# AdaLN block with spectral filter and SwiGLU: a rearranged prologue in place of a staged copy of the edge frequencies

## The chip, the cores and the metric

The kernel runs on one core of a Trainium2 chip. The metric is the device time of one execution in microseconds; the profile's own span (first to last instruction of the program) is 254.3 us where the run took 256.17 us. A core has five engines that this text names: TensorE (PE: matmuls and transposes), VectorE (DVE), ScalarE (ACT), GpSimd (POOL) and SyncE (SP), which here only issues transfers. Transfers (DMA) run on 16 DMA engines beside the compute engines.

## The reference

One token block `x` of 2048 x 640 in bfloat16 goes through two halves, each with a LayerNorm that is scaled and shifted by a vector computed from `c`. The first half filters the whole block in the frequency domain, the second is a SwiGLU feed-forward.

```python
mod = (silu(c) @ w_mod).reshape(1, 6, 1, 640)      # sa, ca, ga, sb, cb, gb
h = layernorm(x) * (1 + ca) + sa
X = rfft2(h, axes=(tokens, model))                 # 2048 x 321 frequencies
y = irfft2(X * (w_r + 1j * w_i), s=(2048, 640))
x = x + ga * y
h = layernorm(x) * (1 + cb) + sb
g = silu(h @ w_gate); u = h @ w_up                 # 640 -> 1728
x = x + gb * ((g * u) @ w_down)
```

## The kernel before

The Fourier transforms are matmuls against cosine and sine tables. The 2048 tokens stand in 16 tiles of 128 rows (`t` = 0..15). For each tile the kernel

- transposes x on TensorE (`t1`) and copies the result from PSUM to SBUF on ACT,
- takes the row statistics (`stats`), for tiles in `BN` with DVE's bn_stats, for the others with a Gram matrix of the transposed tile on TensorE (its diagonal is the sum of squares),
- transforms along the model dimension (`dfwd`), with tables `Rs` that carry the factor 1 + ca,
- subtracts the mean's share on DVE (`zout`), which needs a mean table `Cb`: the transform of a tile of ones,
- scales the token table by 1/std on GpSimd (`gscale`) and transforms along the token dimension (`s1`, lines 398 to 401, "first token matmul" is line 398), and ACT writes the result to `A_sb`.

[...] The start of the program, with the transfers:

```python
    nc.scalar.dma_start(c_row[:], c)
    wmca_v = wm_v[:, :, D:2 * D]
    nc.sync.dma_start(x_sb[:, 0:1, :], x_v[:, 0:1, :])
    nc.sync.dma_start(wm_ca[:, 0:3], wmca_v[:, 0:3])
    nc.scalar.dma_start(Rp[:, 4:5], R_dram[:, 4:5])
    nc.sync.dma_start(wm_ca[:, 3:5], wmca_v[:, 3:5])
    nc.sync.dma_start(Rp[:, 0:4], R_dram[:, 0:4])
    nc.sync.dma_start(x_sb[:, 1:2, :], x_v[:, 1:2, :])
    for xl, xh, gl, gh in ((2, 4, 0, 2), (4, 8, 2, NG9)):
        nc.sync.dma_start(x_sb[:, xl:xh, :], x_v[:, xl:xh, :])
        nc.sync.dma_start(Gtab[:, gl:gh], G_dram[:, gl:gh])
    ...
    def flip_edge(w, f):                                   # row 0 of the flipped table
        ncol = w.ap[0][0]
        nc.sync.dma_start(f[0:1, 0:NT - 1, :], bass.AP(...15 rows of 256...))
        nc.sync.dma_start(f[0:1, NT - 1, :], w[0:1, 65:65 + NW])
    def flip(w, f):                                        # rows 1..127, DRAM to DRAM, 1 MB
        nc.sync.dma_start(f[1:P].rearrange("p k l -> k p l"), bass.AP(...rows reversed...))

    nc.sync.dma_start(x_sb[:, 8:12, :], x_v[:, 8:12, :])
    flip(A_w_i, Wflip[0])
    nc.sync.dma_start(x_sb[:, 12:16, :], x_v[:, 12:16, :])
    flip_edge(A_w_i, Wflip[0])
    flip_edge(A_w_r, Wflip[1])
    flip(A_w_r, Wflip[1])
    nc.sync.dma_start(wm_sa[:], wm_v[:, :, 0:D])
    for i, w in ((0, A_w_i), (2, A_w_r)):
        nc.sync.dma_start(Wn[:, i, :, :], w.rearrange("(k2 k1) l -> k1 k2 l", k1=P)[:, :, 0:NW])
    nc.sync.dma_start(KS2, K_dram[:, 384:576])
    for i in range(2):
        nc.sync.dma_start(Wv[:, 2 * i, :, :], Wflip[i][:])
    nc.sync.dma_start(Ktab[:, 0:384], K_dram[:, 0:384])
    wm_m = wm_v[:, :, 2 * D:6 * D].rearrange("p k (i d) -> p k i d", i=4)
    nc.sync.dma_start(wm_r[:, :, 0, :], wm_m[:, :, 0, :])
```

The filter is needed in natural order (`Wn`) and with its frequencies reversed (`Wv`); the reversed copy is made in DRAM (`Wflip`) and then read back. Row 0 of it comes from other places of the input: these are the edges.

The scale vector and the first tiles:

```python
        t1(0)
        mps = psum[:, 7, 0:NC5]
        mod_cols(mps, wm_ca, range(0, 3))
        mod_cols(mps, wm_ca, range(3, 5))
        nc.vector.tensor_scalar_add(one_p_ca[:], mps, 1.0)
        R1 = Rs[:, 1].rearrange("p (h r) n -> p h (r n)", h=2)
        nc.vector.tensor_scalar_mul(R1[:, 0], R1[:, 0], one_p_ca[:, 4:5])
        nc.vector.tensor_scalar_mul(Rs[:, 0, 0, :], Rp[:, 0, :], one_p_ca[:, 0:1])
        nc.scalar.mul(Rs[:, 0, 1, :], Rp[:, 1, :], one_p_ca[:, 1:2])
        nc.vector.tensor_scalar_mul(R1[:, 1], R1[:, 1], one_p_ca[:, 4:5])
        nc.vector.tensor_scalar_mul(Rs[:, 0, 2, :], Rp[:, 2, :], one_p_ca[:, 2:3])
        nc.scalar.mul(Rs[:, 0, 3, :], Rp[:, 3, :], one_p_ca[:, 3:4])
    idle_pe(IDLE[2])
    t1(1)
    stats(0)
    dfwd(0)
    t1(2)
    stats(1)
    t1(3)
    cbz = zbank(1)
    dft_d(cbz, [ones[:]] * NC5, Rs)                        # mean table, TensorE
    stats(2)
    nc.scalar.mul(Cb[:]..., zview(cbz), 1.0)               # mean table, ACT (line 451)
    gscale(0)
    stats(3)
    zout(0)
    t1(4)
    dfwd(1)
    gscale(1)
    zout(1)
    for t in range(2, NT + 2):
        if t + 3 < NT:
            t1(t + 3)
        if t + 2 < NT:
            stats(t + 2)
        s1(t - 2, Zs.pop(t - 2), Gss.pop(t - 2))
        ...
        if t < NT:
            dfwd(t)
            zout(t)
        ...
```

The middle of the kernel goes over groups of frequencies: A is transposed (by TensorE for the first groups, by DMA transposes for the rest, line 504), transformed over the remaining 16 residues (`stage_a`), multiplied with the filter on DVE (`prod`, line 573), and brought back (`stage_b`, `stage_c`). `evac` copies the result from PSUM to `Em`. Group 4 holds the two edge frequencies 0 and 80:

```python
            B2b = rL.cut(4096 * bi, [16, 128]) if bi < 3 else rM.cut(6144, [16, 128])
            nc.sync.dma_start_transpose(B2b[:, :n, :], A_sb[:, l0:l0 + n, :, :, :].rearrange("p l t c r -> p l (t c r)"))
            for i in range(n):
                B2of[l0 + i] = (B2b, i, l0, n)

        t2_dma(0)
        t2_dma(1)
        t2_dma(2)
        nc.sync.dma_start(wm_r[:, :, 1:3, :], wm_m[:, :, 1:3, :])
        t2_dma(3)
        nc.sync.dma_start(wm_r[:, :, 3, :], wm_m[:, :, 3, :])
        nc.sync.dma_start(Htab[:], H_dram)
        nc.sync.dma_start(RI[:], RI_dram)
        ...
        def evac(u):
            g, l0 = units[u][0], groups[units[u][0]][0]
            if l0 == 0:
                edge = rY.cut(4096, [2, 128])
                nc.scalar.copy(edge[:], banks(6, 1, [4, 128])[:, 0:2, :])       # line 608
                for i in range(2):
                    nc.gpsimd.tensor_copy(Em[:, :, :, 64 * i].rearrange("p v q -> p q v"),
                                          edge[:, i, :].rearrange("p (q v) -> p q v", v=2))   # line 610
            ...
        for g in range(NG + 1):
            ...
            if g + 2 < NG:
                PPs[g + 2] = stage_a(g + 2)[0]     # from group 13 on with modulation matmuls (line 555)
            ...
            for u, gs in enumerate(units):
                if gs[-1] + (1 if gs[0] >= NG - 2 else 3 if gs[0] == 4 else 2) == g:
                    stage_c(u)
                    evac(u)
```

After that come the transform back to tokens, the second LayerNorm and the feed-forward, which the change does not touch.

Of the kernel before, what the change touches and what calls it, by code (L numbers as in the profile page):

```python
# [23 lines left out]
NG9 = 9  # L24
BN = (0, 4, 8, 14)
FLIP = (15, 14, 13, 12, 11, 10, 9)
# [129 lines left out]
def adaln_block_kernel(ctx, tc, A_x, A_w_r, A_w_i, B_x, B_w_gate, B_w_up, B_w_down, c, w_mod, out):  # L156
    nc = tc.nc
# [21 lines left out]
    rY = _Region(big, "rY", 7680, "Y")  # L179
# [31 lines left out]
    wm_ca = rM.cut(0, [NC5, D])  # L211
# [11 lines left out]
    Cb = rE.cut(o, [4, 162], F32); o += 2592  # L223
# [21 lines left out]
    wmca_v = wm_v[:, :, D:2 * D]  # L245
    nc.sync.dma_start(x_sb[:, 0:1, :], x_v[:, 0:1, :])
    nc.sync.dma_start(wm_ca[:, 0:3], wmca_v[:, 0:3])
    nc.scalar.dma_start(Rp[:, 4:5], R_dram[:, 4:5])
    nc.sync.dma_start(wm_ca[:, 3:5], wmca_v[:, 3:5])
    nc.sync.dma_start(Rp[:, 0:4], R_dram[:, 0:4])  # L250
# [22 lines left out]
    nc.sync.dma_start(x_sb[:, 12:16, :], x_v[:, 12:16, :])  # L273
    flip_edge(A_w_i, Wflip[0])
    flip_edge(A_w_r, Wflip[1])
    flip(A_w_r, Wflip[1])
    nc.sync.dma_start(wm_sa[:], wm_v[:, :, 0:D])
    for i, w in ((0, A_w_i), (2, A_w_r)):
        nc.sync.dma_start(Wn[:, i, :, :], w.rearrange("(k2 k1) l -> k1 k2 l", k1=P)[:, :, 0:NW])
    nc.sync.dma_start(KS2, K_dram[:, 384:576])  # L280
    for i in range(2):
# [44 lines left out]
    def zview(zps, M=P):  # L326
        return zps[0:M, :, 0:324]


    if True:  # L330
# [115 lines left out]
        stats(1)  # L446
        t1(3)
        cbz = zbank(1)
        dft_d(cbz, [ones[:]] * NC5, Rs)
        stats(2)  # L450
        nc.scalar.mul(Cb[:].rearrange("p (h r) n -> p h (r n)", h=2), zview(cbz), 1.0)
        gscale(0)
        stats(3)
        zout(0)
        t1(4)
# [3 lines left out]
        for t in range(2, NT + 2):  # L459
# [5 lines left out]
            if t == 14:  # L465
                sps = psum[:, 7, 400:400 + NL]
                for i in range(10):
                    r, c2 = i // 2, i % 2
# [28 lines left out]
    if True:  # L497
# [106 lines left out]
        def evac(u):  # L604
            g, l0 = units[u][0], groups[units[u][0]][0]
            if l0 == 0:
                edge = rY.cut(4096, [2, 128])
                nc.scalar.copy(edge[:], banks(6, 1, [4, 128])[:, 0:2, :])
                for i in range(2):
                    nc.gpsimd.tensor_copy(Em[:, :, :, 64 * i].rearrange("p v q -> p q v"),  # L610
                                          edge[:, i, :].rearrange("p (q v) -> p q v", v=2))
            elif g == NG - 2:
# [54 lines left out]
        for g in range(NG + 1):  # L667
# [16 lines left out]
            for u, gs in enumerate(units):  # L684
                if gs[-1] + (1 if gs[0] >= NG - 2 else 3 if gs[0] == 4 else 2) == g:
                    stage_c(u)
                    evac(u)
# [582 lines left out]
```

## Time and profile before

| | |
|---|---|
| time, median of 3 runs | 256.17 us (255.61 to 256.83) |
| span of the profiled run | 254.3 us, TensorE clock 1.00 |
| busy share: PE, DVE, ACT, POOL | 96%, 82%, 64%, 29% |
| DMA moved | 34.78 MB, mean 137 GB/s |
| forward transform ends (last write of A) | 37.9 us |
| middle, to the first matmul of the way back (line 645) | 65.1 us |
| rest: way back, second LayerNorm, feed-forward | to 254.3 us |

How to read the views: the page gives the busy time of each engine over the whole span and in 40 slices. The timeline lists instructions with start, length, engine, line, output and inputs; in brackets is how long the engine was idle before and what released it. The chain is followed back from the last instruction to what released each step. SPq is SyncE's queue: its entries are the issue of transfers, not the transfers. A landing is the time from issue to the arrival of all of it.

### The profile page before, as it was taken

How to read it: one execution, taken by the hardware profiler on the slowest of the kernel's cores; microseconds unless marked ns; L12 is line 12 of the kernel's file. 1: busy time of each engine (PE TensorE's matmuls, PEld its weight loads, DVE VectorE, ACT ScalarE, POOL GpSimd, SP SyncE). 2: the span in 40 equal slices, each digit the busy share in tenths (PEclk: the TensorE clock that was granted, in tenths of full speed). 3: DMA queues.
4: the chain of work that ended last, by engine and by line, in shares of the span. 5: the costliest groups of instructions: out<-in, count | busy, mean ns of one | idle time of the engine just before them, and what ended most of it. 6: DMA issues, size and time to landing. Idle time of an engine off the chain costs nothing.

```text
span 254.3 us, 6501 instructions
## 1 busy us (share of the span) xinstructions
PE 244.9 (96%) x2520; PEld 199.5 (78%) x2520; DVE 208.0 (82%) x521; ACT 163.7 (64%) x305; POOL 73.6 (29%) x117
## 2 busy tenths in 40 slices
PE   8899987999999999999999999999999999999984
PEld 3788856999788887788877678886668886679953
DVE  2898888888888897979997995879985788994793
ACT  3778656988778698578863477673356766235730
POOL 4387756764021805000004600001430000440021
PEclk9999999999999999999999999999999999999999
DMA  7989999999999899710005120002411000212001
GB/s 222 389 278 336 306 394 190 270 275 390 309 332 281 221 257 156 153 36 0 3 0 106 39 70 8 3 3 52 92 40 35 3 0 4 52 52 59 4 0 52
DMA packets 46588, 34.78 MB, mean 137 GB/s; under 512 B 22111, under 2 KB 43486, under 8 KB 46174
## 3 DMA queue, kind: packets, MB, share of 16 engines
q1 hardware_dynamic: 44892, 30.36, 43.2%
q0 software_dynamic: 1376, 3.93, 6.6%
q8 instruction: 19, 0.31, 0.5%
q10 hardware_dynamic: 290, 0.08, 0.1%
q14 instruction: 11, 0.09, 0.1%
HBM read 26.80 MB, written 4.72 MB: 124 GB/s over the span
## 4 chain that ended last, share of the span: by engine, by line
PE 69%; DVE 5%; ACT 4%; DMA 3%; SPq 2%; issue 1%; DVEq 0%; ACTq 0%
PE psum L1058 29%; PE psum L933 17%; PE psum L1031 8%; DMA rM<-in_w_mod_dram 3%; PE psum L645 3%; SPq L504 2%; PE psum L803 2%; PE psum L580 2%; PE psum L806 2%; PE psum L912 1%; PE psum L551 1%; DVE rA L898 1%; PE psum L601 1%; PE psum L1010 1%; PE psum L650 1%
## 5 line engine op out<-in xcount | busy, mean ns | idle before, releaser
L1058 PEld LDWEIGHTS <-rW 128*128 128x128 bf16 (+1 forms) x528 | 47.0, 98 | 5.9 <-issue 0.6
L949 POOL TENSOR_TENSOR rM<-rM,rL 128x320 f32<-128x320 f32 x7 | 6.2, 885 | 86.4 <-ACT rL L948 86.4
L1058 PE MATMUL psum<-rE,rW 128*128 128x256 f16 (+1 forms) x192 | 27.7, 259 | 0.2 <-ACT rH L1090 0.2
L1058 PE MATMUL psum<-rW 128*128 128x256 bf16 (+1 forms) x240 | 27.1, 259 | 0.0
L1058 PE MATMUL psum<-rY,rW 128*128 128x256 bf16 (+1 forms) x96 | 24.0, 259 | 0.0
L573 DVE TENSOR_TENSOR rM<-psum,rW 128x384 bf16<-128x384 f32 (+2 forms) x42 | 20.4, 542 | 3.7 <-PE psum L551 3.4
L933 PEld LDWEIGHTS <-rX 128*128 128x128 bf16 (+1 forms) x181 | 16.1, 97 | 9.2 <-issue 1.6
L1031 PE MATMUL psum<-rW 128*128 128x256 bf16 (+1 forms) x170 | 23.2, 291 | 0.0
L933 PEld LDWEIGHTS <-rE 128*128 128x128 f16 x168 | 16.4, 98 | 6.5 <-DVE rE L884 0.2
L933 PE MATMUL psum<-rE 128*128 128x320 f16 x126 | 20.4, 299 | 0.0
L933 PE MATMUL psum<-rA,rX 128*128 128x320 bf16 (+1 forms) x119 | 19.5, 301 | 0.8 <-DVE rX L1037 0.8
L1031 PEld LDWEIGHTS <-rW 128*128 128x128 bf16 x170 | 16.6, 98 | 3.8
L1058 PEld LDWEIGHTS <-rE 128*128 128x128 f16 x192 | 17.4, 98 | 2.3
L1108 DVE TENSOR_TENSOR rX<-rH,rL 128x512 bf16<-128x512 bf16 x21 | 8.9, 425 | 11.7 <-ACT rL L1106 11.5
L736 POOL TENSOR_TENSOR rstd<-rstd,mhalf 128x4 f32<-128x4 f32 (+2 forms) x4 | 4.7, 1187 | 44.8 <-DVE rstd L732 44.8
L1098 DVE TENSOR_TENSOR rX<-psum,rX 128x512 f32<-128x512 f32 x21 | 14.4, 688 | 3.2 <-ACT rX L1097 2.9
L1097 ACT COPY rX<-psum 128x512 f32<-128x512 f32 x21 | 12.3, 587 | 7.2 <-PE psum L1058 7.1
L1094 DVE TENSOR_TENSOR rH<-psum,rW 128x512 bf16<-128x512 f32 x21 | 14.5, 690 | 2.4 <-PE psum L1058 0.6
L1090 ACT COPY rH<-psum 128x512 f32<-128x512 f32 x21 | 12.2, 581 | 6.4 <-PE psum L1058 5.7
L1084 ACT COPY rW<-psum 128x512 f32<-128x512 f32 x21 | 12.3, 586 | 5.8 <-PE psum L1058 5.8
L390 DVE SCALAR_TENSOR_TENSOR rE<-rE,mv,psum 128x648 bf16<-128x648 f32 (+1 forms) x17 | 14.1, 841 | 2.0 <-PE psum L323 1.6
L1058 PE MATMUL psum<-rW,rE 128*128 128x256 bf16 (+1 forms) x96 | 15.1, 259 | 0.0
(203 smaller groups left out, 665.5 us busy)
## 6 DMA issues: line engine op xcount, KB each, us to landing
out_dram<-rA SPq DMA_DIRECT2D x31, 80.0 KB, 1.6
rM<-in_w_mod_dram SPq DMA_DIRECT2D x3, 800.0 KB, 9.2
rA<-in_B_w_down_dram SPq DMA_DIRECT2D x1, 2080.0 KB, 12.8
rX<-in_A_x_dram SPq DMA_DIRECT2D x3, 640.0 KB, 7.2
rM<-in_w_mod_dram SPq DMA_DIRECT2D x1, 1600.0 KB, 8.0
rY<-in_B_w_gate_dram POOLq DMA_DIRECT2D x2, 768.0 KB, 6.9
rW<-in_B_w_gate_dram SPq DMA_DIRECT2D x2, 640.0 KB, 7.0
rW<-in_B_w_up_dram SPq DMA_DIRECT2D x2, 640.0 KB, 8.0
```

The costliest lines, as they stand in the source:

```text
L390: nc.vector.scalar_tensor_tensor(Zv[:, h], Cv[:, h], mv[:, t, 0:1], zps[:, h], ALU.mult, ALU.subtract)
L573: nc.vector.tensor_tensor(PP[:, :, hl], xv[:, :, hl], in1, ALU.mult)
L645: nc.tensor.matmul(vps[:, r, :], lhsT=Em[:, v, 4 * t + r, :], rhs=Htab[:, t, v, :], start=(v == 0), stop=(v == 1))
L933: nc.tensor.matmul(o, lhsT=lhsT, rhs=rhs, start=start, stop=stop, skip_group_check=True)
L1031: nc.tensor.matmul(gu[u], lhsT=Wgu[:, u, c5, ff * 128:(ff + 1) * 128], rhs=h2T[:, :, c5, :], start=(c5 == 0), stop=(c5 == NC5 - 1))
L1058: nc.tensor.matmul(o[:, f], lhsT=w, rhs=b, start=(start and f == 0 and i == 0), stop=(stop and f == F - 1 and i == len(ops) - 1), skip_gro ...
L1084: nc.scalar.copy(c0, X)
L1090: nc.scalar.copy(c2, X)
L1094: nc.vector.tensor_tensor(c11, Z, c0, ALU.add)
L1097: nc.scalar.copy(c3, X)
L1098: nc.vector.tensor_tensor(c22, Y, c3, ALU.add)
L1108: nc.vector.tensor_tensor(ato, v4(c11), v4(g21), ALU.mult)
```

## The change

It has five parts.

1. The modulation weights for the scale (`wm_ca`) are issued from two queues, the second part from ACT's, to free SyncE for what follows.
2. The mean table is made ahead of the fourth transpose, and `zout(0)` stands ahead of `stats(3)`, so that the first token matmul can follow sooner.
3. Tile 14 takes its statistics from a Gram matrix, like the other tiles, which takes bn_stats off DVE.
4. The edges of the flipped filter are issued after the natural tables instead of between the flips.
5. The edge frequencies go from PSUM straight to `Em`, one by ACT and one by DVE, with a strided write, in place of one contiguous copy by ACT into SBUF and two strided copies from there by GpSimd; the unit is taken one group earlier.

```diff
@@ -22,7 +22,7 @@
 NC5 = 5
 NFC = 14
 NG9 = 9
-BN = (0, 4, 8, 14)
+BN = (0, 4, 8)
 FLIP = (15, 14, 13, 12, 11, 10, 9)
 EPS = 1e-5
 RC = 162
@@ -244,9 +244,9 @@
     nc.scalar.dma_start(c_row[:], c)
     wmca_v = wm_v[:, :, D:2 * D]
     nc.sync.dma_start(x_sb[:, 0:1, :], x_v[:, 0:1, :])
+    nc.scalar.dma_start(wm_ca[:, 3:5], wmca_v[:, 3:5])
     nc.sync.dma_start(wm_ca[:, 0:3], wmca_v[:, 0:3])
     nc.scalar.dma_start(Rp[:, 4:5], R_dram[:, 4:5])
-    nc.sync.dma_start(wm_ca[:, 3:5], wmca_v[:, 3:5])
     nc.sync.dma_start(Rp[:, 0:4], R_dram[:, 0:4])
     nc.sync.dma_start(x_sb[:, 1:2, :], x_v[:, 1:2, :])
     for xl, xh, gl, gh in ((2, 4, 0, 2), (4, 8, 2, NG9)):
@@ -271,12 +271,12 @@
     nc.sync.dma_start(x_sb[:, 8:12, :], x_v[:, 8:12, :])
     flip(A_w_i, Wflip[0])
     nc.sync.dma_start(x_sb[:, 12:16, :], x_v[:, 12:16, :])
-    flip_edge(A_w_i, Wflip[0])
-    flip_edge(A_w_r, Wflip[1])
     flip(A_w_r, Wflip[1])
     nc.sync.dma_start(wm_sa[:], wm_v[:, :, 0:D])
     for i, w in ((0, A_w_i), (2, A_w_r)):
         nc.sync.dma_start(Wn[:, i, :, :], w.rearrange("(k2 k1) l -> k1 k2 l", k1=P)[:, :, 0:NW])
+    flip_edge(A_w_i, Wflip[0])
+    flip_edge(A_w_r, Wflip[1])
     nc.sync.dma_start(KS2, K_dram[:, 384:576])
     for i in range(2):
         nc.sync.dma_start(Wv[:, 2 * i, :, :], Wflip[i][:])
@@ -444,14 +444,14 @@
         dfwd(0)
         t1(2)
         stats(1)
-        t1(3)
         cbz = zbank(1)
         dft_d(cbz, [ones[:]] * NC5, Rs)
+        nc.scalar.mul(Cb[:].rearrange("p (h r) n -> p h (r n)", h=2), zview(cbz), 1.0)
+        t1(3)
         stats(2)
-        nc.scalar.mul(Cb[:].rearrange("p (h r) n -> p h (r n)", h=2), zview(cbz), 1.0)
         gscale(0)
+        zout(0)
         stats(3)
-        zout(0)
         t1(4)
         dfwd(1)
         gscale(1)
@@ -604,11 +604,9 @@
         def evac(u):
             g, l0 = units[u][0], groups[units[u][0]][0]
             if l0 == 0:
-                edge = rY.cut(4096, [2, 128])
-                nc.scalar.copy(edge[:], banks(6, 1, [4, 128])[:, 0:2, :])
                 for i in range(2):
-                    nc.gpsimd.tensor_copy(Em[:, :, :, 64 * i].rearrange("p v q -> p q v"),
-                                          edge[:, i, :].rearrange("p (q v) -> p q v", v=2))
+                    (nc.scalar.copy, nc.vector.tensor_copy)[i](Em[:, :, :, 64 * i].rearrange("p v q -> p q v"),
+                                   banks(6, 1, [4, 128])[:, i, :].rearrange("p (q v) -> p q v", v=2))
             elif g == NG - 2:
                 nc.vector.tensor_copy(ep_views(l0, 4), banks(1, 1, [4, 128]).rearrange("p i q -> p q i"))
             elif g == NG - 1:
@@ -682,7 +680,7 @@
             if g in (1, 2):
                 ga_mod(320 * (g - 1), 5 + g)
             for u, gs in enumerate(units):
-                if gs[-1] + (1 if gs[0] >= NG - 2 else 3 if gs[0] == 4 else 2) == g:
+                if gs[-1] + (1 if gs[0] >= NG - 2 else 2) == g:
                     stage_c(u)
                     evac(u)
             if g == NG - 1:
```

## The prediction

> **What bounds the kernel now.** I read the page first. TensorE shows 96% busy at full clock, and the chain that ended last is 69% TensorE; its one large entry of another kind is a transfer, 3% of the span. This change touches only the first 50 of 254 us, so the question is which wait ends last there and whether TensorE carries its delay to the end. I read the chain in order of time between 36 and 70 us:
>
> ```profile
> 37.07 0.83 ACT rA L407 x3
> ...
> 39.72 0.74 SPq L504
> ...
> 40.51 2.02 SPq L504
> ...
> 42.58 2.49 SPq L504
> ...
> 45.12 8.00 DMA rM<-in_w_mod_dram
> ...
> 53.17 0.28 PE psum L555 x5
> ```
>
> Columns are start, length and holder. The forward transform ends with the last A table (L407, 37.9 us). SyncE then issues three DMA transposes, 37.74 to 45.07; behind them it issues two modulation blocks (1,600 KB), which land 8.00 us later. From 53.17 on, TensorE runs with hardly a gap. So 53.1 us is a gate: what arrives earlier waits there. The timeline shows how narrow it is:
>
> ```profile
> 53.17 0.28 PE L555 MATMUL psum<-sc_col,rM 128*128 128x1 bf16 x5 [0.26 <-DMA rM<-in_w_mod_dram]
> ```
>
> TensorE was only 0.26 us early (brackets: idle before, releaser). The DVE product that follows at 53.75 had 0.61 us idle. Next, the timeline of the prologue:
>
> ```profile
> 6.42 0.48 PE L313 MATMUL psum<-sc_col,rM 128*128 128x1 bf16 x10 [0.21 <-DMA rM<-in_w_mod_dram]
> 6.94 0.17 DVE L433 TENSOR_SCALAR one_p_ca<-psum 128x5 f32<-128x5 f32 x1 [1.25 <-PE psum L313]
> 7.31 0.41 PE L340 MATMUL psum<-identb,rX 128*128 128x128 bf16 x4 [0.17 <-DMA rX<-in_A_x_dram]
> 9.93 0.72 ACT L451 ACTIVATE rE<-psum 128x648 f32<-128x648 f32 x1
> 12.34 0.30 PE L398 MATMUL psum<-rE 128*128 128x324 bf16 x1 [0.45 <-DVE rE L390]
> ```
>
> The first model transform (L398, tile 0) waits 0.45 us for zout(0) on DVE. From 12.34 to about 29 TensorE repeats every 1.69 us without a gap, so the loop ends as late as it starts. At its end, the last L398 at 36.31 again waits 0.24 us for DVE.
>
> SyncE's own timeline shows the flips and their edges, and the DMA view of 12 to 20 us in 0.2 us slices shows what they do:
>
> ```profile
> 12.60 0.95 SPq L261 DMA_DIRECT2D wflip_i<-in_A_w_i_dram  x1
> 13.61 0.54 SPq L263 DMA_DIRECT2D wflip_i<-in_A_w_i_dram  x1
> 14.19 1.24 SPq L261 DMA_DIRECT2D wflip_r<-in_A_w_r_dram  x1
> 15.47 0.55 SPq L263 DMA_DIRECT2D wflip_r<-in_A_w_r_dram  x1
> 16.07 0.61 SPq L267 DMA_DIRECT2D wflip_r<-in_A_w_r_dram  x1
> 28.86 0.44 SPq L282 DMA_DIRECT2D rW<-wflip_i  x1
> ```
>
> ```profile
> GB/s 315 351 343 353 343 353 343 353 343 353 412 330 371 371 464 425 366 369 379 407 344 264 145 60 53 31 26 67 97 133 205 282 271 302 307 310 310 320 325 346
> ```
>
> Four edge transfers of 7.5 or 0.5 KB hold the queue from 12.60 to 16.07; the second 1 MB flip is issued only then, and from 16.4 to 18.2 the engines run dry, at 26 to 205 GB/s.
>
> [...] one issue here costs 0.35 to 0.5 us, while the 800 KB of scale weights took until 6.4 us. [...] The flipped tables are read back from DRAM (L282), so the edges' landing stands on that path; the edges took 3.6 to 6.0 us from issue to landing. [...] the trace has L608 (ACT, 0.38) and then two L610 (GpSimd, together 1.50).
>
> **The change part by part.**
>
> 1. Scale weights from two queues. It moves one issue (0.49) off SyncE, so x tile 1 is issued some 0.5 earlier. Bytes are unchanged, and the slices there already moved 365 to 384 GB/s. The second part of the weights now shares the engines with the first, so both should land near 6.1 instead of 5.5 and 6.4. But before, 15 of 25 column matmuls (0.64) were done while the second part was on its way. Now all 25 (0.64 + 0.48 = 1.1) may follow 6.1: one_p_ca at 7.2 instead of 6.94. The small R block is issued behind them on ACT, and four DVE operations (0.78) need it. Estimate: 0 to 0.4 us later.
>
> 2. Mean table ahead of the fourth transpose, zout(0) ahead of stats(3). The table's matmuls run from about 8.8 instead of 9.14; ACT evacuates them after copy t1(2), at 9.5 to 10.2 instead of 9.93 to 10.65. zout(0) (0.88) then ends near 11.2 instead of 12.28. But ACT's copy for t1(3), 0.69, now comes second: 10.2 to 10.9 instead of 9.34 to 10.03. gram(3) needs it, and everything on TensorE up to the first L398 stands behind gram(3): it ends near 11.2 instead of 10.32; then t1(4), dfwd(1) and t1(5), 0.3 + 0.55 + 0.3. That gives 12.35 to 12.4, against 12.34. The wait changes its name; the gain is 0.
>
> 3. Tile 14's statistics by Gram matrix. DVE loses 0.88 + 0.21 (bn_stats, aggregate) and gets 0.28 + 0.08 + 0.15; TensorE gets five matmuls, 0.28 in the pipe. Late in the loop TensorE has a 0.22 us wait for GpSimd (L469 on L485, 33.46) which absorbs most of it. Net 0 to 0.1 us later.
>
> 4. Edges issued after the natural tables. The second flip goes out some 2 to 3.5 us sooner and the hole at 16.4 is filled: most DMA engines gain 1.5 us. But the four issues now lie ahead of L282, and their landing, behind the 2 MB of natural tables, releases the read-back. I put that issue near 31 to 32 instead of 28.86: the hole moves rather than goes. The first half of the read-back landed 6.3 us after its issue, at 35.2; the second, another 1 MB at the 400 GB/s of those slices, some 2.6 later, near 37.8. DVE wants it at 40.0 (L414), so a slack of about 2 us should cover the shift. What follows, 800 KB for the gate (L285), leaves the DMA slices at 38.2 now and would leave them between 38 and 39.5, so the transposes issued at 37.74 may start up to 0.7 late.
>
> 5. Edge columns copied straight from PSUM. ACT 0.38 becomes about 0.3, GpSimd loses 1.50, DVE gets some 0.28 in a stretch (46.26 to 51.00) where it never idles, and the unit runs one group earlier. TensorE's wait in front of L601 at 50.27 (0.3) goes. All of this lies ahead of the gate, and 0.28 is less than DVE's 0.61 of idle time: 0.
>
> Sum: A table later by 0.1 to 0.4, transposes later by 0 to 0.7, the rest 0. Taking the middle of the first (0.25) and a small share of the second (0.1), the gate moves by 0.35, and TensorE passes that on: 256.17 + 0.35 = 256.5 us.
>
> **The rivals.** First, the filled hole could win: if the edges land no later than SyncE reaches L282, the tables, the gate's 800 KB and the transposes come up to 0.7 earlier, and the loop start could gain 0.3 if the weights land sooner. Then the gate is at 52.3 to 52.8; TensorE, 0.26 early, and DVE pay part of it back: about 255.5. For it speaks the hole itself, over 1.5 us; against it, that the transposes also wait for L407, which no earlier transfer moves. Second, the read-back becomes the new wait: edges behind a full queue land at 33 or later, the flipped table misses 40.0, DVE stalls and the transposes follow: 257.5 to 258.5. For it speaks the 3.67 us that SyncE spent on one 48 KB issue right behind the natural tables (L280, 25.14 to 28.81), a place that the edges now take. Third, DVE becomes the limit ahead of the gate: +0.28 and a later start exceed 0.61, worth 0.3 us at most.
>
> **Range and chances.** The three runs of before spread over 255.61 to 256.83, so 0.35 us is within their scatter. The first rival sets the lower end, 255.1 with some scatter; the second the upper, 258.1. Two per cent is 5.1 us, more than any term here: within 2% 0.95, slower 0.03 (a stall of the read-back with followers), faster 0.02. On the sign alone I lean slightly to slower.
>
> **What would show it right or wrong.** Right: the first L398 within 0.4 of 12.34, its wait no longer on L390, ACT's fourth copy after the table; no hole at 16 us but one after 28, with L282 issued after 30; L555 at 53.2 to 54.0, still released by the modulation transfer; L608 and L610 gone. Step 2 is wrong if L398 comes before 12.0, step 4 if L282 is issued before 29.5 or DVE waits for the flipped table near 40. The whole is wrong if L555 is released by something other than that transfer, or if the time after it is not as long as before, about 201 us.

## Result and profile after

The changed kernel takes 259.52 us (median of four runs, 258.52 to 259.63) against 256.10 us for the kernel before (255.61 to 256.83): a ratio of 1.0123, 95% interval 1.0087 to 1.0158. That is within 2%, but clearly slower, and above the range of 255.1 to 258.1.

The page of the changed kernel, its head, the busy shares, the granted clock by fortieths of the span, and the engines' shares of the chain that ended last:

```profile
span 256.7 us, 6515 instructions
...
PE 246.6 (96%) x2525; PEld 201.2 (78%) x2525; DVE 207.6 (81%) x521; ACT 164.2 (64%) x305; POOL 71.9 (28%) x115
...
PEclk9799999999999999999999999999999999999999
...
PE 72%; DVE 6%; ACT 4%; issue 1%; DVEq 0%; ACTq 0%
```

Two things are new. The second slice has a granted clock of 0.7, where the page of before shows 9 throughout; and the transfer that held 3% of the chain is gone from it. This traced run was the shortest of the four: its span is 2.4 us longer than that of before (256.7 against 254.3), and its mean granted clock is 0.993, where the other three have 0.998 to 1.00 with spans of 257.1 to 257.9. So the recorded fall of the clock at the start does not go with a longer time. A second trace of the same kernel, below, has a span of 257.4 us.

Where the 2.4 us arise is read from fixed points in the program. All times are in us from the start of the span; "gate" is the first column matmul L555.

| point | before | after | difference |
|---|---|---|---|
| first token matmul (L398) | 12.34 | 13.99 | +1.65 |
| last A table written (L407 ends) | 37.89 | 39.65 | +1.76 |
| read-back of the flipped table issued (L282) | 28.86 | 31.19 | +2.33 |
| gate's transfer issued (L511) | 45.12 | 47.29 | +2.17 |
| gate (L555) | 53.17 | 55.63 | +2.46 |
| first matmul of the way back (L645, after: L643) | 65.09 | 67.55 | +2.46 |
| end of the span | 254.3 | 256.7 | +2.4 |

From the way back on, both take 189.2 us. Everything happens ahead of the gate, and two delays arise independently: one on TensorE in the prologue, one in SyncE's queue. Here is the first, the changed kernel's timeline of 6 to 14 us (start, duration, operation; in brackets the idle time before it and what ended it):

```profile
6.13 0.96 PE L313 MATMUL psum<-sc_col,rM 128*128 128x1 bf16 x25 [0.57 <-DMA rM<-in_w_mod_dram]
6.72 0.78 DVE L425 TENSOR_SCALAR rE<-rE,mask 128x162 bf16<-128x162 bf16 x4 [2.52 <-DMA rE<-tab_R]
...
7.97 0.30 PE L320 MATMUL psum<-rE 128*128 128x324 bf16 x1 [0.36 <-DVE rE L435]
...
12.57 0.47 PE L368 MATMUL psum<-rE 128*128 128x129 bf16 x5 [0.46 <-DVE mv L372]
...
13.99 0.30 PE L398 MATMUL psum<-rE 128*128 128x324 bf16 x1
```

TensorE waits 0.57 us for the weights and does all 25 column matmuls after 6.13; the R block, now behind the weights on ACT's queue, lets DVE begin only at 6.72 instead of 4.91, so the scaled table is 0.36 us late for TensorE. The windows of the same kernel (busy us of PE, PEld, DVE, ACT, POOL; then granted clock, DMA share, GB/s) show what follows:

```profile
6.00:8.00 2.00, 1.51 (x32) 1.32 (x33) 1.24 (x7) 0.68 (x3) 0.00 (x0) 1.00 1.08 400
8.00:10.00 2.00, 2.00 (x17) 1.77 (x17) 1.47 (x6) 1.33 (x4) 0.00 (x0) 0.60 1.02 405
10.00:12.00 2.00, 2.00 (x17) 1.70 (x15) 0.72 (x6) 1.07 (x3) 0.82 (x2) 0.55 1.01 394
```

From 8.4 to 11.8 us TensorE runs at half clock: it is busy for all of the four microseconds from 8 to 12 and completes 34 matmuls, where before completed 54. In narrower windows the granted clock reads 0.50 to 0.52 for these 3.4 us and 1.00 just ahead of them. What made it fall in this execution is not shown: part 1 alone, below, has longer waits in the same places at full clock.

The second delay, in SyncE's queue (start and duration of each issue):

```profile
23.78 3.44 SPq L261 DMA_DIRECT2D wflip_i<-in_A_w_i_dram  x1
27.27 0.53 SPq L263 DMA_DIRECT2D wflip_i<-in_A_w_i_dram  x1
27.84 0.81 SPq L261 DMA_DIRECT2D wflip_r<-in_A_w_r_dram  x1
28.69 0.54 SPq L263 DMA_DIRECT2D wflip_r<-in_A_w_r_dram  x1
...
31.19 0.34 SPq L282 DMA_DIRECT2D rW<-wflip_i  x1
...
32.53 0.74 SPq L285 DMA_DIRECT2D rM<-in_w_mod_dram  x1
39.50 7.75 SPq L504 DMA_TRANSPOSE rL<-rA  x3
47.29 1.38 SPq L511 DMA_DIRECT2D rM<-in_w_mod_dram  x1
```

The first edge, 7.5 KB, holds SyncE for 3.44 us behind the natural tables. That is not the new cost: before, L280 was held there for 3.67 us. New are the other three edge issues, 1.88 us, L280 behind them with 0.58, and a wait of the read-back for the edges to land, until 31.19:

```profile
SPq L282 <- DMA wflip_i<-in_A_w_i_dram: 1.3, 1, 1.3
```

(SyncE's waits: who waited for what, us in total, times, longest.) Less the 0.23 by which the hold is shorter, these make 3.6 us, or 3.7 with the gaps between the issues. SyncE reached this place 1.36 us sooner, at 23.78 instead of 25.14, so 2.33 remain. While the read-back waits the DMA engines are nearly empty: the hole has moved, as the window of 30 to 32 us shows (29 GB/s; before moved 358 there):

```profile
30.00:32.00 2.00, 2.00 (x44) 1.87 (x42) 1.35 (x5) 1.01 (x2) 1.38 (x3) 1.00 0.13 29
```

At the gate the two delays meet. The gate's transfer took 8.3 us from its issue, so it landed at 47.29 + 8.3 = 55.6. TensorE came off its previous matmul at the same moment, and the timeline shows no wait:

```profile
55.47 0.25 PE L551 MATMUL psum<-Ktab,rL 128*128 128x192 bf16 x1
...
55.63 0.28 PE L555 MATMUL psum<-sc_col,rM 128*128 128x1 bf16 x5
```

That is why no transfer stands in the chain, though one is just as late. Either delay hides behind the other; the runs below take them apart.

### The profile page after: what moved, and what is told of

Its sections match the earlier page's. It is cut to its first block, busy times and chain, and to the rows that moved or that the text cites. A ratio compares the mean times of both kernels' runs of the same rounds, so it can differ in the third digit from the quotient of the medians.

```text
span 256.7 us, 6515 instructions
## 1 busy us (share of the span) xinstructions
PE 246.6 (96%) x2525; PEld 201.2 (78%) x2525; DVE 207.6 (81%) x521; ACT 164.2 (64%) x305; POOL 71.9 (28%) x115
## 3 DMA queue, kind: packets, MB, share of 16 engines
HBM read 26.80 MB, written 4.72 MB: 123 GB/s over the span
## 4 chain that ended last, share of the span: by engine, by line
PE 72%; DVE 6%; ACT 4%; issue 1%; DVEq 0%; ACTq 0%
PE psum L1056 29%; PE psum L931 17%; PE psum L1029 8%; PE psum L580 3%; PE psum L643 3%; PE psum L551 3%; PE psum L801 2%; PE psum L804 2%; PE psum L601 1%; PE psum L910 1%; DVE rA L896 1%; PE psum L632 1%; PE psum L1008 1%; DVE rM L573 1%; PE psum L648 1%
## 5 line engine op out<-in xcount | busy, mean ns | idle before, releaser
L1106 DVE TENSOR_TENSOR rX<-rH,rL 128x512 bf16<-128x512 bf16 x21 | 8.9, 425 | 11.7 <-ACT rL L1104 11.6
```

Of the source, the lines that this page charges most:

```text
L1106: nc.vector.tensor_tensor(ato, v4(c11), v4(g21), ALU.mult)
```

## Experiments

The theory after this reading: the late edges delay the gate's transfer, the two queues delay TensorE, and the two overlap rather than add. The rivals: the prologue alone is the cause; the new copies of part 5 are; or the order of the transfers is what matters, so that sending the gate's 800 KB ahead of the read-back would cure it. "Part" is numbered as in the prediction: 1 weights from two queues, 2 mean table, 3 tile 14 by Gram matrix, 4 edges late, 5 edge columns straight from PSUM. The traces' landmarks of the kernels with parts alone or left out (the time is a median; the interval is that of the ratio to the kernel before, whose median was 256.4 to 256.7 us in these groups of runs; three of part 3's twenty runs, of 259.91 us and more, are in its median, which is 256.65 us without them, and not in its ratio; "wait" is TensorE's idle time ahead of the gate, ended by the transfer; 12.34, 45.1, 53.17 with 0.26, and 65.09 are the landmarks of before):

| kernel | time | ratio, 95% | first L398 | gate's transfer issued | gate (wait) | way back |
|---|---|---|---|---|---|---|
| part 1 alone | 257.79 | 1.0014 to 1.0060 | 12.94 | 45.4 | 54.22 (0.73) | 66.14 |
| part 2 alone | 256.92 | 0.9988 to 1.0021 | 12.24 | 45.8 | 54.29 (1.45) | 66.21 |
| part 3 alone | 256.99 | 0.9986 to 1.0037 | 12.26 | 44.7 | 52.70 | 64.63 |
| part 4 alone | 260.45 | 1.0083 to 1.0194 | 12.01 | 48.4 | 56.10 (2.31) | 69.55 |
| part 5 alone | 256.81 | 0.9968 to 1.0015 | 12.27 | 45.4 | 53.98 | 65.90 |
| parts 1 to 4 | 261.63 | 1.0121 to 1.0231 | 15.03 | 50.2 | 57.68 (2.04) | 69.61 |
| whole change, again | 259.37 | 1.0094 to 1.0153 | 13.90 | 48.7 | 56.23 (0.65) | 68.15 |
| without part 1 | 259.51 | 1.0097 to 1.0142 | 12.40 | 49.2 | 56.88 (1.37) | 68.80 |
| without part 4 | 258.42 | 1.0048 to 1.0100 | 12.88 | 45.5 | 54.39 | 66.30 |
| without 1 and 4 | 257.62 | 1.0023 to 1.0064 | 12.16 | 45.1 | 53.72 | 65.63 |

### Each part alone

**Part 1 alone: the weights from two queues.**

```diff
+    nc.scalar.dma_start(wm_ca[:, 3:5], wmca_v[:, 3:5])
     nc.sync.dma_start(wm_ca[:, 0:3], wmca_v[:, 0:3])
     nc.scalar.dma_start(Rp[:, 4:5], R_dram[:, 4:5])
-    nc.sync.dma_start(wm_ca[:, 3:5], wmca_v[:, 3:5])
```

> Part 1 alone: second part of the scale weights from ACT's queue, all else as before. Theory A: TensorE idles about 0.5 us for the weights near 5.6 and 0.4 for the scaled table near 7.6, one_p_ca comes at 7.4 instead of 6.94, the granted clock falls below 0.7 between 8 and 12, and the time rises by 0.5 to 1.7, to 256.6 to 257.8. Theories B and C: the later one_p_ca is 0.4 at most and the time stays within 256.0 to 256.6.

In the traced run the first token matmul comes at 12.94, 0.60 later, with the clock at full: the column matmuls and DVE's work on the R block come late, as in the whole change. The waits here are longer than in the trace of the whole change (0.86 and 0.51 us against 0.57 and 0.36), and yet the clock held. It did not hold in every execution: 9 of the 20 have a mean granted clock of 0.993, which is what one stretch of 3.4 us at half clock takes off 256 us, and a median time of 258.07 us, against 257.12 for the other 11. So the rise of 0.4% is a mixture. The 0.60 us are a third of the 1.65 in the whole change; the rest there goes with the half clock, since with the clock full ("the changed kernel with its start filled", below) the same matmul comes at 12.91.

**Part 2 alone: the mean table ahead of the fourth transpose.**

```diff
-        t1(3)
         cbz = zbank(1)
         dft_d(cbz, [ones[:]] * NC5, Rs)
+        nc.scalar.mul(Cb[:]..., zview(cbz), 1.0)
+        t1(3)
         stats(2)
-        nc.scalar.mul(Cb[:]..., zview(cbz), 1.0)
         gscale(0)
+        zout(0)
         stats(3)
-        zout(0)
```

> Part 2 alone: mean table ahead of the fourth transpose, zout(0) ahead of stats(3). As predicted: the first L398 at 12.3 to 12.4, no longer released by L390, and no change of the time, 256.0 to 256.8. Rival: zout(0) a full microsecond earlier brings the first L398 to 11.3 to 11.8 and the time to 255.4 to 256.0.

TensorE's timeline in that kernel:

```profile
10.82 0.47 PE L368 MATMUL psum<-rE 128*128 128x129 bf16 x5 [0.82 <-ACT rE L343]
...
12.24 0.30 PE L398 MATMUL psum<-rE 128*128 128x324 bf16 x1
```

The wait has changed place, from zout on DVE (0.45) to the Gram matrix of tile 3 behind ACT's copy (0.82), and 0.10 us is gained at the first token matmul. No difference in the time can be measured.

**Part 3 alone: tile 14 by Gram matrix** (`BN = (0, 4, 8)`).

> Part 3 alone: statistics of tile 14 by the Gram matrix. As predicted: last L398 at 36.3 to 36.5 and no change of the time, 256.0 to 256.8. Rival: DVE's relief of 0.6 us shortens the end of the loop, last L398 at 36.0 or earlier.

The last token matmul stands at 36.22 instead of 36.31 and the time is the same within its interval.

**Part 4 alone: the edges after the natural tables.**

```diff
-    flip_edge(A_w_i, Wflip[0])
-    flip_edge(A_w_r, Wflip[1])
     flip(A_w_r, Wflip[1])
     ...  (scale weights, natural tables)
+    flip_edge(A_w_i, Wflip[0])
+    flip_edge(A_w_r, Wflip[1])
```

> Part 4 alone: edge transfers of the flipped table after the natural tables. Theory A: no effect on the first L398 (12.3) and 256.0 to 256.7. Theory C: read-back issued near 31 instead of 28.9, the 800 KB for the gate land near 42 instead of 40.2, the DMA transposes and the gate's transfer follow by 1 to 2 us, L555 at 54 to 55 with TensorE waiting for the transfer for 1 us or more, time 257.0 to 258.3. Theory B: 256.1.

Alone it costs as much as the whole change: 260.45 us. The queue of SyncE, and the gate:

```profile
23.19 4.03 SPq L261 DMA_DIRECT2D wflip_i<-in_A_w_i_dram  x1
...
31.19 0.34 SPq L282 DMA_DIRECT2D rW<-wflip_i  x1
...
33.99 0.43 SPq L285 DMA_DIRECT2D rM<-in_w_mod_dram  x1
37.39 10.94 SPq L504 DMA_TRANSPOSE rL<-rA  x3
48.37 0.58 SPq L511 DMA_DIRECT2D rM<-in_w_mod_dram  x1
```

```profile
53.55 0.25 PE L551 MATMUL psum<-Ktab,rL 128*128 128x192 bf16 x1
56.10 0.28 PE L555 MATMUL psum<-sc_col,rM 128*128 128x1 bf16 x5 [2.31 <-DMA rM<-in_w_mod_dram]
```

The A table is ready as early as before (37.54), and the first transpose is issued at 37.39, but the three take 10.94 us instead of 7.33. The second is issued only at 42.1; the 800 KB ahead of it in the queue landed at 33.99 + 8.4 = 42.4. In the kernel before that pair is 40.5 and 40.2, in the changed kernel 42.3 and 42.3. So with the read-back issued 2.33 us later the 800 KB land 2.2 later, the three transposes take 3.61 longer, and the gate's transfer goes out 3.25 us late. TensorE, on time, waits 2.31 us. That wait costs more than its length, as the windows of the same kernel show (columns as above):

```profile
54.00:56.00 2.00, 0.00 (x0) 0.00 (x0) 0.03 (x1) 0.85 (x1) 1.06 (x2) 1.00 1.12 315
56.00:58.00 2.00, 1.90 (x27) 1.87 (x28) 1.02 (x2) 0.58 (x1) 0.14 (x1) 0.70 1.08 212
58.00:60.00 2.00, 2.00 (x25) 1.98 (x23) 1.02 (x2) 0.82 (x2) 0.27 (x1) 0.50 0.93 302
```

From 56.8 to 60.2 the clock is half (all four executions have a mean granted clock of 0.992 or 0.993), and the stretch from the gate to the way back takes 13.45 us instead of 11.92. Gate +2.93 and clock +1.53 make 4.46; the way back starts at 69.55, 4.46 after that of before.

**Part 5 alone: the edge columns straight from PSUM** (ACT and DVE each copy one 128 x 128 block into elements 256 bytes apart, in place of ACT's contiguous copy and GpSimd's two scatters; one group earlier).

> Part 5 alone: edge frequencies copied straight from PSUM by ACT and DVE and one group earlier; prologue as before. Theory A: at most 0.5 over before, 256.1 to 256.8, since the gate's transfer at 53.1 hides most of it. Theory B: the 1.5 us that DVE loses (0.80 waiting for ACT's copy, 0.74 copying) less its 0.61 of idle time at the gate, so 257.0 to 258.6. Theory C: 256.1 to 256.5.

Both copies are slower than I had put them. ACT's takes 0.76 us and DVE's 0.74, and DVE has waited 0.80 us for ACT's, though they write different columns: the two follow one another. The lines here are from the changed kernel, where the same happens:

```profile
50.89 0.76 ACT L608 CAST rE<-psum 128x128 bf16<-128x128 f32 x1
...
51.69 0.74 DVE L608 CAST rE<-psum 128x128 bf16<-128x128 f32 x1 [0.80 <-ACT rE L608]
...
53.32 0.49 PE L551 MATMUL psum<-Ktab,rL 128*128 128x192 bf16 x4 [0.29 <-DVE rM L573]
```

In the run of part 5 alone the gate is at 53.98 without a wait, 0.81 later than before. The transfer landed there at 45.43 + 8.5 = 53.9, so this run doesn't tell which of the two set it. The last matmul ahead of the gate starts about 1.0 us later than before, at 53.63, and at 53.64 in the kernel without parts 1 and 4, where the transfer had landed at 52.9. Before, and then that kernel:

```profile
52.66 0.25 PE L551 MATMUL psum<-Ktab,rL 128*128 128x192 bf16 x1
```

```profile
53.64 0.25 PE L551 MATMUL psum<-Ktab,rL 128*128 128x192 bf16 x1
```

Yet the time of part 5 alone is the same within 0.3%. The traced run of before was a short one (span 254.3; the median span of the runs of before in this group is 254.8), and without part 5 the gate stood anywhere between 52.70 (part 3 alone) and 54.29 (part 2 alone), with the landing of its transfer. Whether it is the copies or the unit's place one group earlier that makes TensorE late was not tried apart.

### Parts left out

**Parts 1 to 4, without part 5.**

> Parts 1 to 4 alone; the edge frequencies stay staged as before. Theory A (the first token matmul starts late because TensorE stood idle for the weights and was then granted a low clock, and TensorE carries that to the end): first L398 near 14.1, gate (first L555) near 55, time 257.8 to 258.8. Theory B (the straight edge copies, 0.76 on ACT and then 0.74 on DVE, one after the other, cost the time): 256.0 to 256.6. Theory C (the edge transfers hold back the read-back and so the gate's transfer): 258.3 to 259.3, with L555 released by that transfer at 55.5 whatever TensorE did before.

This kernel has both delays at their worst. The weights landed so late that TensorE waited 2.10 us for them (L313 at 7.54), the clock was half from 8.2 to 11.6, the first token matmul came at 15.03; and still TensorE waited 2.04 us at the gate: the transposes go out with the end of the A table, which is late here (37.74 with its end at 37.89 before, 39.50 and 39.65 in the changed kernel), and the transfer behind them was issued at 50.2. Taking part 5 away brings nothing back; the time is 2.1 us above that of the whole change. The start of this kernel is the same program as that of the whole change; why the weights came 1.4 us later is not known. After its wait of 2.04 us at the gate the clock stayed at 1.00.

**The whole change, traced a second time, without part 1, and without part 4.** The edits of part 1 and part 4 above are undone in the changed kernel, one at a time.

> The changed kernel once more, unaltered, to see how far one profile speaks for all. Both theories: 258.5 to 260.5. Theory D (two delays in series: the start of the token transform comes late, and the gate's transfer comes late; whichever ends last sets the gate, and a TensorE that had to wait runs the next 3.4 us at half clock): last L398 between 36.5 and 39, first L555 between 55.5 and 57, and a clock of 0.5 for one stretch of 3.4 us either near 8 to 12 or right after L555. Rival E (the delays simply add): L555 at 53.2 plus the delay of the last L398 plus 3.

> The changed kernel with the scale weights issued as before (parts 2 to 5 stay). Theory D: the first L398 back at 12.0 to 12.5 with full clock from 5 to 50, but the gate's transfer still lands at 55.5 to 56.2, TensorE waits for it 1.5 us or more and drops to half clock after it: no gain, 259 to 260.5. Rival E: the 1.7 us of late start come back, 257.3 to 258.

> The changed kernel with the edge transfers of the flipped table between the flips as before (parts 1, 2, 3, 5 stay). Theory D: the read-back is issued at 28.9 again; the gate's transfer follows the end of the A table by 15.2, and only the late start remains, 0.6 us if TensorE keeps its clock through the prologue and 1.7 if it does not: L555 at 54 to 55.3, time 257 to 258.4. Rival E: the 3 us of the late edges come back in full: 255.8 to 256.8.

In the second trace of the whole change the first token matmul is as late as in the first (13.90), and the mean granted clock is 0.998, which leaves room for about 1 us at half clock (an estimate: 0.002 of the span of 257.4 us is 0.5 us lost). The lengths of the matmuls say otherwise:

```profile
5.25 0.63 PE L340 MATMUL psum<-identb,rX 128*128 128x128 bf16 x4
...
9.07 0.63 PE L340 MATMUL psum<-identb,rX 128*128 128x128 bf16 x4
...
10.94 0.38 PE L340 MATMUL psum<-identb,rX 128*128 128x128 bf16 x4
```

Four transposes take 0.63 us in the half-clock stretch of the first trace and 0.39 at full clock in both kernels. So here TensorE ran slowly from 5.25 to about 10.6 us, far longer than the record of the clock accounts for; in this trace the lengths show what the record does not.

Without part 1 the prologue is that of before (12.40, full clock all along), and nothing is gained: 259.51 us. TensorE is 1.5 us earlier and spends 1.37 of it waiting at the gate for the transfer, which is issued at 49.2. Without part 4 the transfer is issued at 45.5, as before, and 0.5% is gained; now TensorE is what comes late (gate at 54.39, no wait). In this run, the shortest of its four, part 1 delayed the start by 0.54, and the clock was full from about 5.8 on (four transposes took 0.63 us at 5.22 and 0.41 at 7.09). This is the overlap: each delay hides behind the other, and the late transfer is the longer of the two.

**Without parts 1 and 4.**

> Parts 2, 3 and 5, without parts 1 and 4. If the two delays are all of it: first L398 at 12.2 to 12.4, full clock, read-back issued at 28.9, L555 at 53.2 to 54.2, time 256.2 to 257.2, the same as before. If something else in parts 2, 3 or 5 costs: 257.5 or more.

The first token matmul (12.16) and the gate's transfer (issued 45.1) are those of before. 0.44% remains, 0.23 to 0.64: TensorE reaches the gate at 53.72 with no wait, behind part 5's copies. Each of the three parts alone had shown no measurable difference (0.9992, 1.0005, 1.0011). Why their sum is 1.1 us is not settled: the traced run was one of the short ones (span 254.8, the median of the twenty is 255.65, of before 254.7), so its gate, 0.55 late, accounts for half; a run in which the two copies do not wait for each other was not made.

### The clock and the queue

**Part 4 with TensorE kept busy at the gate.** If the half clock is TensorE's own doing, small matmuls in its wait should cure it and nothing else. They write to columns of PSUM that nothing reads.

```diff
+                if g == NG - 8 and i == 0:
+                    for _ in range(22):
+                        nc.tensor.matmul(psum[:, 2 + 2 * (g % 2), 200:256], lhsT=ones[:],
+                                         rhs=ones[:, 0:56], start=True, stop=True)
```

> Part 4 alone again, with 22 small matmuls on a matrix of ones ahead of the first L555, whose result nobody reads: TensorE has something to do while it waits for the gate's transfer. Theory D: L555 at 56 as without them, but the clock stays at 1.0 after it and the stretch from L555 to the way back shrinks by 1.5 us: 258.4 to 259.4 against 260.45 for part 4 alone. Rival: the low clock has another cause than the wait, then 260 to 261.

```profile
54.00:56.00 2.00, 0.44 (x17) 0.32 (x13) 0.11 (x1) 0.93 (x2) 0.99 (x2) 1.00 1.12 295
56.00:58.00 2.00, 1.91 (x37) 1.92 (x38) 1.33 (x3) 0.59 (x1) 0.22 (x1) 1.00 1.12 221
58.00:60.00 2.00, 2.00 (x44) 2.00 (x42) 1.70 (x5) 1.93 (x3) 0.60 (x2) 1.00 0.89 301
```

The gate is where it was in part 4 alone (56.09 against 56.10), the 22 matmuls take 0.73 us of the wait and leave 1.65 of it, the clock stays at 1.00, and the way back starts at 68.01 instead of 69.55: 1.54 us, the whole cost of the half clock. The median is 259.1 against 260.45; one of the four runs took 262.15 us with a mean granted clock of 0.992, so the filler does not help every time, but the other three have 1.00, where all four of part 4 alone have 0.992 or 0.993.

**The changed kernel with its start filled.** Two more idle matmuls of 512 columns ahead of the column matmuls, one more behind them.

```diff
-IDLE = (3, 6, 1, 2)
+IDLE = (3, 6, 2, 2)
     ...
+        idle_pe(2)
         mod_cols(mps, wm_ca, range(0, 3))
```

> The changed kernel with two more matmuls of 512 columns ahead of the 25 column matmuls and one more behind them, which write a bank nobody reads: TensorE idles less while the weights come. If the idle time makes the low clock: clock 1.0 from 5 us on, first L398 at 12.7 to 13.1 instead of 13.9 to 14.0; the time stays at 258.8 to 260, since the gate's transfer lands at 55.6 or later anyway. If the weights alone make the late start: first L398 at 13.8 or later.

The half clock is gone in this trace (four transposes take 0.39 us from 4.80 on), and the first token matmul comes at 12.91 instead of 13.99. The time is 259.79 us, ratio 1.0125 (1.0079 to 1.0172), as without it: the gate's transfer is issued at 48.8 and TensorE waits for it 1.02 us. The start was not what held the changed kernel.

**Part 4 with the order mended.** If the read-back's place in the queue were at fault, the gate's 800 KB and the remaining tables could go ahead of it and fill the hole.

```diff
     nc.sync.dma_start(KS2, K_dram[:, 384:576])
-    for i in range(2):
-        nc.sync.dma_start(Wv[:, 2 * i, :, :], Wflip[i][:])
-    nc.sync.dma_start(Ktab[:, 0:384], K_dram[:, 0:384])
     nc.sync.dma_start(wm_r[:, :, 0, :], wm_m[:, :, 0, :])
+    nc.sync.dma_start(Ktab[:, 0:384], K_dram[:, 0:384])
+    for i in range(2):
+        nc.sync.dma_start(Wv[:, 2 * i, :, :], Wflip[i][:])
```

> Part 4 alone, but the 800 KB for the gate vector and the inverse tables are issued ahead of the read-back, so that they move while SyncE waits for the edges to land. Theory D (what costs the time is the hole in the queue between the natural tables and the read-back, which pushes those 800 KB and with them the DMA transposes back): the 800 KB land near 36 instead of 42.4, the read-back near 39 to 40, the three transposes take 7 to 8 us instead of 10.9, L555 at 52.9 to 54, time 255.8 to 257. Rival F (the edge transfers themselves are slow behind a full queue and whatever is issued after them lands late, in any order): L555 at 55 or later, 258.5 to 260.5.

SyncE's queue, and then DVE and TensorE at 42 to 44 us:

```profile
23.76 4.72 SPq L261 DMA_DIRECT2D wflip_i<-in_A_w_i_dram  x1
...
31.17 0.42 SPq L282 DMA_DIRECT2D rM<-in_w_mod_dram  x1
...
34.01 0.38 SPq L285 DMA_DIRECT2D rW<-wflip_r  x1
```

```profile
42.37 0.43 DVE L414 TENSOR_TENSOR rW<-rW 128x512 bf16<-128x512 bf16 x1 [2.59 <-DMA rW<-wflip_r]
...
43.44 0.80 PE L551 MATMUL psum<-Ktab,rM 128*128 128x192 bf16 x4 [3.92 <-DVE rM L573]
```

(L282 is the 800 KB here, L285 the read-back.) The 800 KB now go out at 31.17, which is later than in the kernel before (30.3), because the edge held SyncE for 4.72 us and the four edge issues end at 30.49. They landed at 36.7, yet the second transpose started at 42.0, behind the read-back. And the flipped table misses its use: DVE waits 2.59 us, TensorE 3.92, and its clock is half from 42.6 to 49.4. The time is 260.15 us, so this order is no cure. Part of it is the clock: the one execution at full clock took 258.53 us with a span of 255.8, the traced one lost some 3.4 us in 6.8 at half clock.

**The kernel before with the edges issued by GpSimd.** If SyncE's time is what the edges cost, another issuer should free it.

```diff
-        nc.sync.dma_start(f[0:1, 0:NT - 1, :], bass.AP(...))
-        nc.sync.dma_start(f[0:1, NT - 1, :], w[0:1, 65:65 + NW])
+        nc.gpsimd.dma_start(f[0:1, 0:NT - 1, :], bass.AP(...))
+        nc.gpsimd.dma_start(f[0:1, NT - 1, :], w[0:1, 65:65 + NW])
```

> The kernel before with its four edge transfers issued by GpSimd instead of SyncE, in the same place of the program. Theory D: SyncE issues the second flip near 12.6, the hole at 16.4 goes, nothing new waits: the read-back is issued at 27 to 28.9, the 800 KB land near 39, L555 at 52.5 to 53.2 and then TensorE or DVE bounds this stretch, 255.4 to 256.4. Rival: GpSimd's transfers land so late that the read-back waits for them too, 257 or more.

```profile
12.58 0.57 SPq L267 DMA_DIRECT2D wflip_r<-in_A_w_r_dram  x1
...
24.29 3.35 SPq L280 DMA_DIRECT2D Ktab<-tab_K  x1
27.82 0.33 SPq L282 DMA_DIRECT2D rW<-wflip_i  x1
...
44.61 0.91 SPq L511 DMA_DIRECT2D rM<-in_w_mod_dram  x1
```

The second flip goes out 3.5 us sooner, the read-back 1.04, the gate's transfer 0.5. But that transfer then takes 8.4 us instead of 8.0, the gate stands at 53.10, and the time is 256.3 us (ratio 0.9973 to 1.0007). What part 4 was meant to bring, an earlier flip and no hole at 16 us, is had here without its cost, and it is worth nothing measurable. The 3.35 us now fall on L280, as in the kernel before: in each of the seven traces in which that place was read, it held what was issued there, for 3.34 to 4.72 us.

### Two tries at a gain

Both start from the kernel before and try to bring the first token matmul forward: part 2, and `t1(4)`, `dfwd(1)` and `gscale(1)` moved ahead of `stats(3)`, so that TensorE has work while ACT copies. The first also has part 3 and GpSimd's edges.

```diff
         gscale(0)
         zout(0)
-        stats(3)
         t1(4)
         dfwd(1)
         gscale(1)
+        stats(3)
```

> The kernel before with parts 2 and 3, with tile 3's statistics moved behind t1(4) and dfwd(1) so that TensorE does not stand behind ACT's fourth copy, and with the four edge transfers issued by GpSimd. If the start and SyncE's queue are what sets the gate: first L398 at 11.4 to 11.8, A ends at 37.0 to 37.3, L555 at 52.2 to 53, time 255.0 to 255.9. If the gate's transfer does not follow: 256 to 256.8.

> The same earlier start without part 3 and with the edge transfers on SyncE as before. If the transposes start with the end of A: L555 0.7 earlier, 255.3 to 256.1. If they wait for the 800 KB in front of them, which leave the engines at 38.2: no gain, 256 to 256.8.

Neither gains: 256.91 us (0.9993 to 1.0026) and 256.52 us (0.9973 to 1.0018), with the first token matmul at 12.86 and 12.56, later than before. In the first of them the moved transposes meet a new wait, for DVE's read of the Gram matrix (L372):

```profile
10.83 0.38 PE L340 MATMUL psum<-identb,rX 128*128 128x128 bf16 x4 [0.46 <-DVE mv L372]
...
12.58 0.38 PE L340 MATMUL psum<-identb,rX 128*128 128x128 bf16 x4 [0.46 <-DVE mv L372]
```

No kernel of this study measurably beat the one before.

## Why the prediction was wrong

The outline held: the sign was right, nothing behind the gate changed (from it to the end of the span both kernels take 201.1 us: 254.3 less 53.17 and 256.7 less 55.63), the hole moved from 16 us to 30, the read-back went out at 31.19 where I had put it "near 31 to 32", and DVE did not wait for the flipped table. What failed is the size of two terms.

**Step 4, the term "the transposes issued at 37.74 may start up to 0.7 late", of which the sum took 0.1.** This is the main error. I read from the DMA slices that the 800 KB leave them "at 38.2 now and would leave them between 38 and 39.5". The slices do fall off there (378 GB/s from 37.5 to 38.0 us, 184 in the next half), but the trace of before counts 9.9 us from L285's issue to the landing, so it landed at 40.2, and the second transpose went out right after it, at 40.51: there was no slack to use up. In the changed kernel the landing is at 42.3, 2.1 later, because L285 went out 2.2 later and took as long as ever (9.8 us). I had the read-back's delay right and passed it on in part, when it goes on in full. The second transpose waited with it. Part 4 alone moved the issue of the gate's transfer by 3.25 us, in the changed kernel by 2.17. What the traces show is that the second transpose's issue and the landing of what was queued ahead of it coincide within 0.4 us in three kernels (40.51 and 40.2 before, 42.3 and 42.3 in the changed kernel, 42.1 and 42.4 in part 4 alone); that the one waits for the other is inferred from this and from the kernel with the mended order, not shown by itself.

The second rival had the right place: the edges behind the natural tables delay the read-back and what follows. The 3.67 us of L280 that it names are not the cost, since the first edge was held 3.44 us in place of them; the further issues and the landing are. Its size of 257.5 to 258.5 is nearer the result, but its path was wrong: DVE never stalled for the flipped table in the changed kernel. The delay went through the queue to the gate, and I had not put it into the sum. My figure of 0.35 to 0.5 us for an issue fits the first ones of the queue only; later ones in the same trace took 5.41 (L273) and 4.62 us (L279).

**Step 1, "0 to 0.4 us later".** Alone it cost 0.60. In the changed kernel it cost 1.65, of which about 1.05 go with a stretch at half clock. I didn't consider the clock, since the page of before showed it full. When it falls is not settled: waits of 0.57 and 0.36 us went with the fall in one kernel, waits of 0.86 and 0.51 in part 1 alone did not in the traced run, and 9 of that kernel's 20 executions have the lower mean. This error hardly entered the time: taking part 1 out of the changed kernel left 259.51 us.

**The half clock at a wait.** The same omission in the other place: where TensorE did wait at the gate for 2.31 us, 1.53 us came on top. Waits of 1.37, 1.45 and 2.04 us at the same place, in the kernels without part 1, with part 2 alone and with parts 1 to 4, left the clock full; one of 3.92 us ahead of the gate, in the kernel with the mended order, went with 6.8 us at half clock. These runs don't show what decides it.

**Step 5, "0".** I put the copies at 0.3 and 0.28; they took 0.76 and 0.74, one after the other. The wait of TensorE ahead of L601 at 50.27, which I expected to go, I had misread: the 0.24 us of the view are those of the weight loads, and the matmuls of before have a gap of about 0.1. The changed kernel has a wait of 0.32 there, at 50.57, behind a copy by ACT. TensorE's last matmul ahead of the gate comes about 1.0 us later (53.64 against 52.66). In the changed kernel most of that hides behind the late transfer; in the kernel without parts 1 and 4 it is the likeliest part of the 0.44% that remain, which no run isolates.

**Steps 2 and 3** were right: the wait changed its name, and neither moved the time.

**The first rival**, that the filled hole would win, falls with the run in which GpSimd issued the edges: the flip and the read-back came 3.5 and 1.0 us sooner and the gate did not move.

So the account of the traced run is: the transfer's delay puts the gate at 55.6, TensorE's own delays (1.76 at the end of the loop and about 1.0 from part 5; its last matmul ahead of the gate is 2.81 later, 55.47 against 52.66) put it at about the same time, and the gate moves by 2.46 us. The second trace has the transfer later (issued 48.7) and the gate at 56.23, 3.06 later than before, with a span 3.1 longer.

## What to carry to other kernels

In these traces a small transfer cost its place in SyncE's queue, not its bytes: the same 7.5 KB edge held the queue for 0.95 us between the flips and for 3.44 behind the natural tables. Before moving one, look at what it adds at the new place (here three more issues and a wait of 1.3 us for the landing; the hold behind the two large tables was paid before as well) and at everything that stands behind it, down to the transfer that the gate waits for. Where two delays end at one gate, undo them one at a time and together, since either alone may show nothing. And at each new wait on TensorE ask whether the clock will hold, because the wait can then cost more than its length (here 1.53 us on top of 2.31).

## What was not expected of the hardware

- Whatever SyncE issued directly behind the two natural-table loads was held, in the seven traces read there: a 7.5 KB edge 3.44 to 4.72 us in four, the 48 KB of L280 3.34 to 3.67 us in three. The edge issues behind that first one took 0.53 to 0.81.
- The clock fell to half for 3.4 us after a wait of 2.31 us at the gate, not after one of 2.04; with 22 matmuls of 56 columns in such a wait (0.73 us, 1.65 left) it has a mean of 1.00 in three executions of four and 0.992 in the fourth. At the start 9 of 20 executions of one kernel have the mean clock of such a stretch and 11 don't.
- One trace has a mean granted clock of 0.998, about 1 us at half clock, while the matmuls from 5.25 to about 10.6 us have the lengths of the half clock (0.63 us for four transposes against 0.39).
- The same three DMA transposes took between 6.93 and 11.30 us. Apart from the kernel with the mended order (9.45), the later the 800 KB queued ahead of them landed, counted from the first transpose's issue, the longer they took, but for differences of a few tenths: 6.93 us with the landing 1.2 after that issue, 7.33 with 2.5, 9.32 with 3.4, 11.30 with 5.1.
- A copy of 128 x 128 from PSUM into elements 256 bytes apart took 0.76 us on ACT and 0.74 on DVE, twice what ACT needed before for 128 x 256 into contiguous columns (0.38).
